# A four-layer network and its gradients on one core: a float32 second operand for the derivative, dS transposes placed anew, identity transposes where layers meet

## The chip, the cores and the metric

The kernel runs on one core of a Trainium2 chip, in one launch. The metric is the device time in microseconds; the time before is the median of four runs.

## The reference

Four residual layers, A, B, A, B, over a sequence of S = 2048 rows of D = 640 in bfloat16, with H = 32 heads of 20. The two A layers share their weights, and so do the two B layers. The kernel returns the network's output, the gradient of its input, and the gradients of the four weight matrices, given the gradient of the output.

```python
def A(x, wqkv, wo):                      # linear attention
    q, k, v = split(x @ wqkv)            # heads of 20
    phi = lambda t: where(t > 0, t + 1, exp(t)) + 1e-6
    pq, pk = phi(q), phi(k)
    kv = einsum("bhsd,bhse->bhde", pk, v)
    z = einsum("bhsd->bhd", pk)
    o = einsum("bhqd,bhde->bhqe", pq, kv) / (einsum("bhqd,bhd->bhq", pq, z)[..., None] + 1e-6)
    return merge(o) @ wo

def B(x, wqkv, wo):                      # causal softmax attention, window of 256
    q, k, v = split(x @ wqkv)
    s = where((i - j >= 0) & (i - j < 256), einsum("bhqd,bhkd->bhqk", q, k) * 20 ** -0.5, -1e9)
    return merge(einsum("bhqk,bhkd->bhqd", softmax(s), v)) @ wo

x = x + A(layernorm(x), A_wqkv, A_wo)    # layer 0
x = x + B(layernorm(x), B_wqkv, B_wo)    # layer 1
x = x + A(layernorm(x), A_wqkv, A_wo)    # layer 2
x = x + B(layernorm(x), B_wqkv, B_wo)    # layer 3
# returned: x, and by jax.vjp with grad_out: dx, dA_wqkv, dA_wo, dB_wqkv, dB_wo
```

## The kernel before

**Stages.** The sequence is cut into 16 tiles of 128 rows. The order of everything on PE, DVE, ACT and POOL is the order of the program; a hand-written plan gives each step a place (a number of slots), the steps are sorted by it and run slot by slot. DMAs all go through the SP queue, which the compiler orders itself. Measured from the span's start, the stages are: the forward pass up to about 688 us; the core of layer 3's gradients, 689 to 1160; layer 2's linear gradients ("linear stage"), 1163 to 1296; the core of layer 1, 1296 to 1768; layer 0's linear gradients mixed with the products for the weight gradients, to 2040; the rest of the weight gradients.

**PLACES.** One table holds the places. `f1`, `f2`, `f3` are steps of the forward pass (normalisation, dense products, features); `bf` is what goes before a core's chunk (`plan_before`: the product of the incoming gradient with Wo, its mask by the softmax's denominator, and the transposes `dT` of L796 and their copies L797); `bh` is what goes behind it (`plan_behind`: the transposes of dq, dk, dv by DMA, the product with the weights, the layer norm's gradient `ln` and `ln2`, the next layer's `dn`, L874 to L904, and the products `outer`); `l2` is one tile of the linear stage (`plan_linear`); `n1` starts layer 1's core inside the linear stage of layer 2. `xx` and `bd` have an entry for each of 32 units and are described next.

**The core.** A core goes through 8 chunks of two tiles; a chunk has 32 units (a tile, four heads, two of them at a time). In each step of `core_step`, a new unit's scores `s` are made (PE, 32-row products, L138 like all products) and its `e = exp(s)` (ACT, L662), masked by POOL (L674, L678); the unit three steps back gets `dp` (PE) and `ds = dp * e` (DVE, L665); the unit four steps back has its `ds` transposed; and the unit seven steps back (`lag`) enters the accumulators `acc` (PE), which read `ds`, `e` and the transposed `dsT`. The transposes take one of two ways. By PE: six transposes into a PSUM tile `flip` (L685) and one copy to `dsT`, on ACT (L690) or DVE (L692). By DMA: one DMA transpose, issued by SP at L108 as soon as `ds` is there. Which way is decided by

```python
    def by_dma(n):
        return n >= 64 and PLACES["bd"][n % 32] == 1
```

and which engine copies by a running count of both engines' work, `on_act`, whose result `xx` inverts from unit 64 on. `thin` is a number of transposes of the identity matrix (`warm`) that are put into a step ahead of the transposes, so that two successive steps have at least `FULL = 3600` columns of PE work:

```python
            k = min(6, max(0, -((cols[n] + cols[n + 1] - self.FULL) // 128)))
            m = n + 1 if not self.by_dma(n - 3) else n
            thin[m] += k
```

The first 64 units of a core have at least `WARM = (6, 4)` of them; they have no transposes by DMA. The last 12 slots of the forward pass up to `END` have `TAIL = 5` each. After `END` the remaining slots of the forward pass run as `hooks` inside the core's first steps.

**The linear stage.** `plan_linear` is run for 16 tiles, 8 slots apart. Its steps in the order of the entries of `l2`: `load` (five loads for two tiles: `ldn`, `lv`, `lpqk`, `lhn`, `lg`); `turn` of dn, v, pk (PE transposes and a copy, L162 and L165 or L167); `part` twice for each of dn, v, pk (products with the 20x21 blocks of the state, and for dn and v the derivative of phi); `turn_q` (a transpose `dqT<-dqa` by DMA); `turn_kv` twice (PE transposes L983, copies L986, L988); six parts of `dh` (products with the weights, closed on ACT, L1001); `ln` (DVE L1009 and L1011, POOL L1012) and `ln2` (ACT L1018, POOL L1019, and for each second tile the store of `lgn`, which is the gradient handed to the next layer). The derivative `fd`, which is min(pqk - 1e-6, 1), is L969, and its product with the PSUM tile is L971:

```python
                nc.vector.scalar_tensor_tensor(out=f, in0=src("pq" if nm == "dn" else "pk")[:, c * CW:(c + 1) * CW], scalar=-EPS,
                                               in1=self.one.to_broadcast([P, CW]), op0=ALU.add, op1=ALU.min)
                nc.vector.tensor_tensor(out=dst, in0=ps[:, 0:CW], in1=f, op=ALU.mult)
```

Layer 1's first `plan_before` (loads of `g<-lgn`, L772 and L779 to L789, the transposes L796) is woven into the end of that stage, from slot `b0` on.

Of the kernel before, what the change touches and what calls it, by code (L numbers as in the profile page):

```python
# [13 lines left out]
BF = mybir.dt.bfloat16  # L14
F32 = mybir.dt.float32
P = 128
# [5 lines left out]
TT = T // P  # L22
DT = D // P
G = H // 4
# [15 lines left out]

PLACES = dict(
    f1=[0.1, 1.7, 2.5, 6.6, 9.6, 12, 13.2, 14.1, 14.5, 14.6, 14.5, 16.1],
    f2=[-27.5, -23.6, -21.5, -20.6, -19.5, -17.9, -16.5, -15.1, -13.5, -7.8, -6.9, -5.5, -4.7, -3.8, -2.9, 11, 12, 13, 14, 17.6, 22.4, 23.3, 24, 25.1, 26.4, 27.3],
    f3=[-35.7, -30, -26.5, -25, -24, -23.8, -22.5, -18, -16.4, -14, -12.1, -7.4, -6.8, -6, -4.9, -3.5, -1.7, 11.3, 12.4, 13.4],
    bf=[2.1, 3.1, 5.2, 14.9, 17.9, 6.2, 7.8, 10, 14.6, 28.3],
    bh=[13.1, 14.5, 15.5, 17.1, 17.5, 18, 20, 21.2, 25.7, 28.3, 30, 36, 19.1, 20.1, 21.8, 22.5, 23.3, 24.6, 25.2, 27.5, 30.5, 31.7, 33, 35, 41.5, 43, 2.2, 8.3, 9.5, 12, 18.9, 34.5],
    l2=[-10.4, -1.3, 0.6, 1.2, 1.9, 3.2, 4.6, 6.2, 7, 7.5, 5, 8, 8.3, 10.2, 11.8, 14, 14.4, 15.4, 16, 16.2, 18.7],
    n1=[9.7, 0.5, 3.3, 3.6, 5.3, 9, 3, 4.7, 5.4, 5.6, 24],
    xx=[1, 1, 0, 0, 0, 0, 1, 1, 0, 0, 0, 0, 0, 1, 0, 0, 1, 0, 0, 0, 0, 0, 0, 1, 0, 0, 1, 0, 0, 0, 1, 0],
    bd=[0, 0, 1, 0, 0, 0, 1, 0, 0, 0, 0, 0, 0, 1, 1, 0, 0, 1, 1, 0, 1, 0, 1, 0, 1, 0, 1, 1, 0, 1, 1, 0])  # L50


class Kern:
    def __init__(self, ctx, tc, x0, A_w, A_wo, B_w, B_wo, grad, outs):
        self.ctx, self.tc = ctx, tc
        self.nc = nc = tc.nc
        self.W = dict(A=A_w, B=B_w)
        self.Wo = dict(A=A_wo, B=B_wo)
        self.grad = grad
        self.out_x4, self.out_gx, dWA, dWoA, dWB, dWoB = outs  # L60
        self.dW = dict(A=dWA, B=dWB)
        self.dWo = dict(A=dWoA, B=dWoB)
        self.serial = 0

        dram = ctx.enter_context(tc.tile_pool(name="dram", bufs=1, space=bass.MemoryType.DRAM))
        const = ctx.enter_context(tc.tile_pool(name="const", bufs=1))

        def d(name, shape, dt=BF):
            return dram.tile(shape, dt, name=name)

        self.hn = [d(f"hn{l}", [T, D]) for l in range(4)]
        self.dq = [d(f"dqkv{l}", [T, QT]) for l in range(4)]
        self.o = [d(f"o{l}", [T, D]) for l in range(4)]
        self.x2 = d("x2", [T, D])
        self.WTA, self.WoTB = d("WTAt", [P, NF * D]), d("WoTBt", [P, DT * D])
        self.x0 = x0
        self.gs = [d(f"g{l}", [T, D]) for l in range(3)] + [grad]
        self.sv = {}
        for l in (0, 2):
            self.sv[l] = dict(pqk=d(f"pqk{l}", [T, 2 * D]), v=d(f"v{l}", [T, DA]),  # L80
                              dn=d(f"dn{l}", [T, DA]))
        for l in (1, 3):
            self.sv[l] = {k: d(f"{k}{l}", [TT, P, 3, G * P]) for k in ("s", "T")}

        self.ident = const.tile([P, P], BF, name="ident")
        make_identity(nc, self.ident)
        self.bm = const.tile([KB, HB, HA], BF, name="bm")
        nc.gpsimd.memset(self.bm, 1.0)
        nc.gpsimd.affine_select(out=self.bm, in_=self.bm, compare_op=ALU.is_ge, fill=0.0, base=0,
                                pattern=[[-DH, HB], [0, HA]], channel_multiplier=1)  # L90
        nc.gpsimd.affine_select(out=self.bm, in_=self.bm, compare_op=ALU.is_ge, fill=0.0, base=DH - 1,
                                pattern=[[DH, HB], [0, HA]], channel_multiplier=-1)
        self.mhalf = const.tile([P, 1], F32, name="mhalf")
        nc.gpsimd.memset(self.mhalf, -0.5)
        self.rs = [const.tile([P, TT], F32, name=f"rs{l}") for l in range(4)]
        self.r = [const.tile([P, TT, H], F32, name=f"r{l}") for l in range(4)]
        self.mz = {l: const.tile([KB, 6, KA], BF, name=f"mz{l}") for l in (0, 2)}
        self.mzT = {l: const.tile([KA, 6, KB], BF, name=f"mzT{l}") for l in (0, 2)}
        self.one = const.tile([P, 1], BF, name="one")
        nc.gpsimd.memset(self.one, 1.0)  # L100
        self.dmz = const.tile([KB, 6, KA], BF, name="dmz")
        self.dmzT = const.tile([KA, 6, KB], BF, name="dmzT")
        self.macc = const.tile([KB, 6, KA], F32, name="macc")
# [133 lines left out]
    def forward(self, st):  # L237
# [48 lines left out]
        B1, B3, F = 138, 302, 6  # L286
        END = B3 + G * TT
        plan = []
# [15 lines left out]
        c1, c3 = 118, B1 + 144  # L304
# [36 lines left out]
        slots = [[f for a, f in plan if int(a) == n] for n in range(int(plan[-1][0]) + 1)]  # L341

        def run(n):
            u, fs = None, slots[n]
            if B1 <= n < B1 + G * TT:
                if n == B1:
                    for f in fs:
                        f()
                    fs = []
                u = self.f_scores(st, *divmod(n - B1, G), X[1])  # L350
            elif B3 <= n < END:
                u = self.f_scores(st, *divmod(n - B3, G), X[3])
            for f in fs:
                f()
            if END - 12 <= n < END:
                self.warm(self.TAIL, st.ps.tile([P, 8, P], BF, name="warm", tag="m"))
            if u is not None:
                self.f_masks(*u)
                st.pend.append((l0(n), *u))
            if len(st.pend) > (st.behind if u is not None else 0):  # L360
                self.b_pv(st, *st.pend.pop(0))

        def l0(n):
            return 1 if n < B3 else 3
        for n in range(END):
            run(n)
        st.pSs.close()
        return [lambda n=n: run(n) for n in range(END, len(slots))], keep

    def f_scores(self, st, t, g, X):  # L370
# [263 lines left out]
        return n >= 64 and PLACES["bd"][n % 32] == 1  # L634

    WARM = (6, 4)
    TAIL = 5
    FULL = 3600

# [505 lines left out]
    def core(self, st, l, g_out, B, hooks):  # L1145
# [37 lines left out]
        for n in range(64):  # L1183
            thin[n] = max(thin[n], self.WARM[n // 32])
        n = 0
# [36 lines left out]
    def passes(self):  # L1222
# [5 lines left out]
        st = S()  # L1228
        with ExitStack() as rest:
# [17 lines left out]
            left3 = self.core(st, 3, self.gs[2], st.core, hooks)  # L1247
# [3 lines left out]
            left3 = left3[8:]  # L1251
# [13 lines left out]
            plan = [(a, lambda f=f: f and f()) for a, f in enumerate(left3)] + [(20, next_pools)]  # L1265
# [9 lines left out]
                self.core_slabs(1, B)  # L1275
            b0 = base + 8 * (TT - 1) + PLACES["n1"][0]
            plan.append((b0, begin))
            fs = self.plan_before(st, 1, 0, B, (PLACES["n1"][1:6], PLACES["n1"][6:11]), -10, True)
            plan += [(b0 + a, f) for a, f, *_ in fs if a < 20]
            hooks = self.slots([(a - 20, f) for a, f, *_ in fs if a >= 20], 8)  # L1280
# [51 lines left out]
            with ExitStack() as es, ExitStack() as le:  # L1332
# [8 lines left out]
                X, plan = {}, []  # L1341
# [70 lines left out]
```

The softmax here doesn't subtract the row's maximum and nothing guards it: scores larger than these inputs give would overflow.

## Time and profile before

| | |
|---|---|
| Median of four runs | 2255.18 us (2252.42 to 2258.45) |
| The profiled execution | 2253.89 us, its span 2252.2 us |
| PE busy | 2077.6 us |
| DVE, ACT, POOL busy | 1454.4, 1357.6, 1092.4 us |
| Identity transposes in the core (`thin`, L173) | 906 |
| Identity transposes at the forward pass's end (`warm`, L173) | 60 |
| dS transposes on PE (L685) / by DMA | 1944 / 156 |

PE is TensorE's matmul, PEld its weight load, DVE VectorE, ACT ScalarE, POOL GpSimd, SP the queue of DMA issues. In the slices each digit is a fortieth of the span, in tenths; PEclk is the clock granted to TensorE in tenths of full speed. In a table of windows each row is one stretch: its length, busy time and instruction count of each engine, the granted clock, the mean busy share of the 16 DMA engines, and GB/s. In the waits a row reads: engine and line, what it waited for, microseconds in total, times, the longest. In the groups: line, engine, operation, names and shapes, count, then busy time in us and mean ns of one, then idle time before.

### The profile page before, as it was taken

The numbers are of one execution on the slowest core, as the hardware profiler recorded it, in microseconds if no ns is written. First come the engines' busy times: TensorE is split into PE (matmuls) and PEld (weight loads), VectorE is DVE, ScalarE is ACT, GpSimd is POOL, SyncE is SP. The second block draws the span as 40 slices with busy tenths as digits, with TensorE's granted clock in tenths as the row PEclk, the third lists the DMA queues.
The fourth block names the chain that finished last, engine by engine and source line by source line (L and its number), as shares of the span: only waits on it lengthen the run. The fifth ranks groups of instructions, "written<-read, shape, count | busy, mean of one in ns | idle before, by whom it ended". The sixth has DMA issues, their size and how long they took to land. (4 is left out here: it accounts for less than half of the span.)

```text
span 2252.2 us, 76829 instructions
## 1 busy us (share of the span) xinstructions
PE 2077.6 (92%) x32061; PEld 1693.2 (75%) x32061; DVE 1454.4 (65%) x2934; ACT 1357.6 (60%) x2109; POOL 1092.4 (49%) x1888
## 2 busy tenths in 40 slices
PE   7889998899989999998979889999988899999999
PEld 5667776577767877777757678777776788889998
DVE  6778885777744788887749858788776245550000
ACT  5467887377776888887737668888876233430000
POOL 2046665156666677777634456777774312220000
PEclk9999999999999999999999989999999999999999
DMA  7488785698879598998799733999997998857753
GB/s 260 142 232 231 224 223 152 159 223 217 205 211 235 151 183 202 211 206 185 157 282 263 203 97 101 205 211 205 202 183 171 270 292 248 247 165 199 201 143 90
DMA packets 721357, 449.50 MB, mean 200 GB/s; under 512 B 461296, under 2 KB 697840, under 8 KB 720624
## 3 DMA queue, kind: packets, MB, share of 16 engines
q1 hardware_dynamic: 721008, 444.58, 78.2%
q8 instruction: 251, 4.11, 0.8%
q14 instruction: 98, 0.80, 0.1%
HBM read 213.09 MB, written 149.82 MB: 161 GB/s over the span
## 5 line engine op out<-in xcount | busy, mean ns | idle before, releaser
L665 DVE TENSOR_TENSOR ds<-dp,e 128x768 bf16<-128x768 f32 (+2 forms) x512 | 463.9, 906 | 175.1 <-PE s L138 61.7
L662 ACT ACTIVATE e<-s 128x768 bf16<-128x768 f32 (+2 forms) x512 | 395.6, 773 | 137.5 <-PE s L138 105.1
L385 ACT ACTIVATE eT<-sT 128x1536 bf16<-128x1536 f32 (+2 forms) x256 | 351.1, 1372 | 130.7 <-PE sT L138 129.3
L138 PE MATMUL wg<-rhs,lhs 128*128 128x240 bf16 (+1 forms) x3840 | 374.4, 256 | 8.3 <-DMA lhs<-o 6.9
L138 PEld LDWEIGHTS <-lhs 128*128 128x128 bf16 x3840 | 337.8, 98 | 23.3 <-DMA lhs<-o 8.1
L674 POOL TENSOR_SCALAR_AFFINE_SELECT e<-e 128x256 bf16<-128x256 bf16 x512 | 208.3, 409 | 249.4 <-ACT e L662 244.0
L138 PEld LDWEIGHTS <-dqT 128*128 128x128 bf16 x1920 | 171.1, 98 | 63.2 <-issue 10.4
L391 POOL TENSOR_SCALAR_AFFINE_SELECT eT<-eT 128x512 bf16<-128x512 bf16 x256 | 162.9, 637 | 108.9 <-ACT eT L385 107.2
L138 PE MATMUL acc<-slabqs,ds 128*128 128x20 bf16 x2880 | 210.1, 172 | 1.4 <-ACT dq L744 0.5
L138 PE MATMUL dp<-slabvT,dT 32*128 32x384 bf16 (+2 forms) x1024 | 167.8, 320 | 44.5 <-DVE ds L665 39.6
L138 PE MATMUL acc<-ds,e 128*128 128x20 bf16 x2880 | 208.1, 171 | 0.0
L678 POOL TENSOR_SCALAR_AFFINE_SELECT e<-e 128x256 bf16<-128x256 bf16 x448 | 197.3, 440 | 0.0
L138 PEld LDWEIGHTS <-ds 128*128 128x128 bf16 x2880 | 188.0, 96 | 11.8 <-issue 3.5
L138 PEld LDWEIGHTS <-e 128*128 128x128 bf16 x2880 | 170.2, 96 | 10.8 <-issue 1.8
L1012 POOL TENSOR_TENSOR dh<-dh,lg 128x640 f32<-128x640 f32 x32 | 51.5, 1610 | 256.7 <-DVE s L1009 256.7
L685 PE MATMUL flip<-ident,ds 128*128 128x128 bf16 x1944 | 169.8, 221 | 3.3 <-DVE ds L772 1.2
L138 PE MATMUL s<-slabkT,slabqT 32*128 32x384 bf16 (+2 forms) x1024 | 167.9, 323 | 4.6 <-ACT dT L797 3.3
L1094 DVE CAST wr<-wg 128x240 bf16<-128x240 f32 (+1 forms) x72 | 27.2, 377 | 222.1 <-PE wg L138 213.6
L1092 ACT CAST wr<-wg 128x240 bf16<-128x240 f32 (+1 forms) x48 | 16.3, 339 | 254.8 <-PE wg L138 223.4
L138 PE MATMUL dense<-WB,hnT 128*128 128x320 bf16 x960 | 166.2, 305 | 3.4 <-DVE o L459 2.0
L138 PE MATMUL dense<-WTA,dqT 128*128 128x320 bf16 x960 | 162.9, 301 | 1.4 <-DMA dqT<-dqa 1.0
L138 PE MATMUL acc<-slabks,dsT 128*128 128x20 bf16 x2880 | 147.2, 171 | 12.7 <-DMA dsT<-ds 12.6
(176 smaller groups left out, 4604.4 us busy)
## 6 DMA issues: line engine op xcount, KB each, us to landing
rhs<-dqkv SPq DMA_DIRECT2D x64, 480.0 KB, 5.0
s<-s SPq DMA_DIRECT2D x32, 768.0 KB, 3.9
T<-T SPq DMA_DIRECT2D x32, 768.0 KB, 3.9
dqkv<-dq SPq DMA_DIRECT2D x16, 960.0 KB, 5.7
dqkv<-dqa SPq DMA_DIRECT2D x32, 480.0 KB, 4.6
slabkT<-T SPq DMA_DIRECT2D x56, 256.0 KB, 4.5
slabvT<-T SPq DMA_DIRECT2D x56, 256.0 KB, 4.1
slabks<-s SPq DMA_DIRECT2D x56, 256.0 KB, 3.8
```

Of the source, the lines that this page charges most:

```text
L138: return self.nc.tensor.matmul(out, lhsT=lhsT, rhs=rhs, start=start, stop=stop, skip_group_check=True, **kw)
L385: nc.scalar.activation(e[:, :, 0:nb * P], s[:, :, 0:nb * P], ACT.Exp)
L391: nc.gpsimd.affine_select(out=dg, in_=dg, compare_op=ALU.is_ge, fill=0.0, base=0, pattern=[[0, 4], [1, P]], channel_multiplier=-1)
L662: nc.scalar.activation(u.e[:, :, 0:u.cw], s[:, :, 0:u.cw], ACT.Exp)
L665: nc.vector.tensor_tensor(out=d.ds[:, :, 0:d.cw], in0=d.dp[:, :, 0:d.cw], in1=d.e[:, :, 0:d.cw], op=ALU.mult)
L674: nc.gpsimd.affine_select(out=dg, in_=dg, compare_op=ALU.is_ge, fill=0.0, base=0, pattern=[[0, 2], [-1, P]], channel_multiplier=1)
L678: nc.gpsimd.affine_select(out=fr, in_=fr, compare_op=ALU.is_ge, fill=0.0, base=-1, pattern=[[0, 2], [1, P]], channel_multiplier=-1)
L685: nc.tensor.transpose(ps[:, 3 * j + i, :], f.ds[:, j, i * P:(i + 1) * P], self.ident)
L1012: nc.gpsimd.tensor_tensor(out=x["dh"], in0=x["dh"], in1=L["g"][:, i, :], op=ALU.add)
L1092: nc.scalar.copy(o[:, 0:w], ps[:, 0:w])
L1094: nc.vector.tensor_copy(o[:, 0:w], ps[:, 0:w])
```

## The change

Three things change at once.

1. The table `PLACES`: entries of `f2`, `f3`, `bf`, `bh`, `l2`, `n1`, and the flags `xx` and `bd`. `bd` has 15 units of 32 by DMA in the place of 13: units 6 and 17 go back to PE, units 5, 11, 16 and 28 go to DMA, so that 26 to 30 are all by DMA. Counted in the program: 180 DMA transposes of dS (156 before), 1800 PE transposes of dS (1944), 940 `thin` transposes (906).
2. `self.one`, the second operand of L969, is float32 in the place of bfloat16.
3. `HOLD`: identity transposes, 8 in a slot, in three places where one layer's work meets the next: the slots after the end of the forward pass (the first steps of layer 3's core), the slots around the beginning of layer 2's linear stage (from four before the end of layer 3's left-over steps to three behind it), and seven slots from `b0` + 3.95 at the end of that stage. The first two entries of `HOLD` are 0 and put nothing in. The program has 228 `warm` transposes, 60 before.

```diff
 PLACES = dict(
-    f2=[-27.5, -23.6, -21.5, -20.6, -19.5, -17.9, -16.5, -15.1, -13.5, -7.8, -6.9, -5.5, -4.7, -3.8, -2.9, 11, 12, 13, 14, 17.6, 22.4, 23.3, 24, 25.1, 26.4, 27.3],
-    f3=[-35.7, -30, -26.5, -25, -24, -23.8, -22.5, -18, -16.4, -14, -12.1, -7.4, -6.8, -6, -4.9, -3.5, -1.7, 11.3, 12.4, 13.4],
-    bf=[2.1, 3.1, 5.2, 14.9, 17.9, 6.2, 7.8, 10, 14.6, 28.3],
-    bh=[13.1, 14.5, 15.5, 17.1, 17.5, 18, 20, 21.2, 25.7, 28.3, 30, 36, 19.1, 20.1, 21.8, 22.5, 23.3, 24.6, 25.2, 27.5, 30.5, 31.7, 33, 35, 41.5, 43, 2.2, 8.3, 9.5, 12, 18.9, 34.5],
-    l2=[-10.4, -1.3, 0.6, 1.2, 1.9, 3.2, 4.6, 6.2, 7, 7.5, 5, 8, 8.3, 10.2, 11.8, 14, 14.4, 15.4, 16, 16.2, 18.7],
-    n1=[9.7, 0.5, 3.3, 3.6, 5.3, 9, 3, 4.7, 5.4, 5.6, 24],
-    xx=[1, 1, 0, 0, 0, 0, 1, 1, 0, 0, 0, 0, 0, 1, 0, 0, 1, 0, 0, 0, 0, 0, 0, 1, 0, 0, 1, 0, 0, 0, 1, 0],
-    bd=[0, 0, 1, 0, 0, 0, 1, 0, 0, 0, 0, 0, 0, 1, 1, 0, 0, 1, 1, 0, 1, 0, 1, 0, 1, 0, 1, 1, 0, 1, 1, 0])
+    f2=[-26.3, -23.6, -21.5, -20.6, -19.5, -17.4, -16.5, -15.4, -13.5, -7.8, -6.9, -5.5, -4.8, -3.8, -2.9, 11, 12.5, 13, 14, 17.6, 22.4, 23.2, 24.1, 25.1, 26.5, 27.3],
+    f3=[-35.7, -29.4, -26.6, -25, -24, -23.8, -22.2, -18, -16.4, -15, -12.1, -7.7, -6.8, -6, -4.4, -3.4, -1.7, 11.3, 12.4, 13.4],
+    bf=[2.6, 3.1, 5.2, 12.9, 17.7, 6.7, 9.3, 10.5, 16.6, 29.3],
+    bh=[13.1, 14.6, 15.8, 17.1, 17.5, 18, 20, 21.2, 25.7, 28.3, 30, 36, 19.6, 20.1, 21.8, 22.5, 23.3, 24.6, 25.2, 27.5, 30.5, 31.7, 33, 35, 41.5, 43, 2.2, 8.3, 10.5, 11, 19.9, 34.5],
+    l2=[-12.4, -0.6, -3.8, 2.7, 1.3, 3.1, 4.6, 6.2, 6.7, 7.6, 5.3, 8.1, 8.1, 9.7, 11.8, 14, 14.7, 16, 17.1, 18.9, 20.5],
+    n1=[9.6, 0, 2.4, 3.7, 4.5, 6.1, 0.5, 5.5, 5.8, 6.6, 24.3],
+    xx=[1, 1, 1, 0, 0, 1, 1, 1, 0, 1, 0, 0, 0, 1, 0, 0, 0, 0, 0, 0, 0, 0, 0, 0, 1, 0, 1, 0, 0, 0, 1, 0],
+    bd=[0, 0, 1, 0, 0, 1, 0, 0, 0, 0, 0, 1, 0, 1, 1, 0, 1, 0, 1, 0, 1, 0, 1, 0, 1, 0, 1, 1, 1, 1, 1, 0])
...
-        self.one = const.tile([P, 1], BF, name="one")
+        self.one = const.tile([P, 1], F32, name="one")
...
+            for a, b, k in ((c1 - 2, B1, self.HOLD[0]), (B1 + G * TT, B3, self.HOLD[1]), (END, len(slots), self.HOLD[2])):
+                if a <= n < b and k:
+                    self.warm(k, st.ps.tile([P, 8, P], BF, name="warm", tag="m"))
             for f in fs:
...
     WARM = (6, 4)
+    HOLD = (0, 0, 8, 8, 8)
     TAIL = 5
...
+            def hold(k):
+                self.warm(k, st.ps.tile([P, 8, P], BF, name="warm", tag="m"))
+            plan += [(len(left3) + a, lambda: hold(self.HOLD[3])) for a in range(-4, 4)]
+            plan += [(b0 + a + 0.95, lambda: hold(self.HOLD[4])) for a in range(3, 10)]
             fs = self.plan_before(st, 1, 0, B, (PLACES["n1"][1:6], PLACES["n1"][6:11]), -10, True)
```

## The prediction

> **What bounds the kernel now.** I read the head of the page and the slices first.
>
> ```profile
> span 2252.2 us, 76829 instructions
> ...
> PE 2077.6 (92%) x32061; PEld 1693.2 (75%) x32061; DVE 1454.4 (65%) x2934; ACT 1357.6 (60%) x2109; POOL 1092.4 (49%) x1888
> ...
> PE   7889998899989999998979889999988899999999
> ...
> PEclk9999999999999999999999989999999999999999
> DMA  7488785698879598998799733999997998857753
> ```
>
> PE carries 92% of the span and every slice. Its clock falls in one slice only, the one where layer 2's gradients hand over to layer 1's core. Next, the table of windows: a steady chunk of each core, the first 10.2 us of layer 3's core, the linear stage of layer 2, the first 13.7 us of layer 1's core, the linear stage of layer 0.
>
> ```profile
> core 0: us, PE busy (x) PEld busy (x) DVE busy (x) ACT busy (x) POOL busy (x), PEclk, DMA share, GB/s
> 876.27:931.81 55.54, 51.48 (x988) 41.14 (x986) 44.87 (x67) 44.95 (x76) 42.63 (x83) 1.00 0.95 203
> 688.70:698.90 10.20, 8.94 (x77) 5.75 (x78) 3.18 (x8) 4.21 (x8) 4.25 (x9) 0.50 0.71 162
> 1185.00:1283.00 98.00, 92.29 (x1066) 73.62 (x1063) 92.45 (x175) 67.44 (x137) 44.78 (x32) 1.00 0.86 234
> 1296.30:1310.00 13.70, 10.10 (x76) 6.67 (x75) 3.51 (x8) 5.31 (x10) 6.84 (x10) 0.50 0.21 62
> 1483.61:1538.77 55.16, 51.48 (x988) 41.13 (x986) 44.89 (x68) 44.97 (x76) 42.65 (x83) 1.00 1.03 213
> 1850.00:2040.00 190.00, 190.00 (x2042) 169.69 (x2041) 99.18 (x193) 73.67 (x153) 46.22 (x30) 1.00 0.74 209
> ```
>
> So PE sets the chunks (51.5 of 55.5 us) with 4 us of gaps, and the DMA engines stand near 1.0 beside it. Both cores begin at half clock. In layer 0's linear stage PE has no gap at all. Third, the waits: 850 to 1070 us (four lines), then 1283 to 1312 us (one line), then PE's alone from 1290 to 1312 us (one line).
>
> ```profile
> PE dp L138 <- DVE ds L665: 10.7, 27, 0.9
> PE acc L138 <- DMA dsT<-ds: 5.2, 5, 2.9
> DVE ds L665 <- DMA dsT<-ds: 5.0, 2, 3.4
> DVE ds L665 <- ACT dsT L690: 1.8, 3, 0.6
> ...
> DVE ds L665 <- DMA g<-lgn: 9.4, 1, 9.4
> ...
> PE s L138 <- ACT dT L797: 3.3, 1, 3.3
> ```
>
> In the core, PE waits for `ds`, seldom for a DMA transpose. At the hand-over it waits for `dT`, and `ds` for the store of `lgn`. Fourth, the groups by form.
>
> ```profile
> L690 ACT COPY dsT<-flip 128x768 bf16<-128x768 bf16 x158 | 126.4, 800 | 0.3
> L969 DVE SCALAR_TENSOR_TENSOR fd<-lpqk,one 128x320 bf16<-128x320 bf16 x128 | 101.5, 793 | 0.0
> L692 DVE COPY dsT<-flip 128x768 bf16<-128x768 bf16 x134 | 73.3, 547 | 0.0
> ```
>
> L969 takes 793 ns on average, 482 ns in the median (the tile view), so (793 - 482) x 128 = 40 us of it is standing still.
>
> **Transposes of dS (bd, xx, bf, bh).** There are 8 chunks of 32 units per core and `bd` counts from unit 64, so it acts on 6 chunks of each core. Per chunk 15 units instead of 13 go by DMA: 144 PE transposes go in the program, and the fill-up to FULL adds 34, net -110. Eight transposes back to back took 0.62 us in the timeline (L983 at 1283.82), the first 0.22 (its group's mean), so 0.057 us each: -6.3 us, 0.5 a chunk, as far as PE bounds. Copies: with the new `xx`, ACT makes 7 instead of 11 (-4 x 0.800 = -3.2 us), DVE 10 instead of 8 (+2 x 0.547 = +1.1 us, to 46.0 of 55.5). DVE stays under PE; what I charge it is later `ds`, what ACT gives back is earlier `e`, and I set these against each other. SP gets 24 issues of 1.2 us more, 2.5 us a chunk. Three further DMAs (the second `turn`, `store`, `load_o`) move by one unit of 1.73 us, and the entries of `bf` by up to two; they keep their order towards the units that read them, so I charge nothing, and if one came late the price is a wait like `PE acc <- DMA`, about 1 us a chunk. Taken: -0.5 us a chunk, **-6 us**. Good bound: half of PE's wait for `ds` (10.7 us over 4 chunks' 220 us, so 1.35 a chunk) goes too, -1.8 a chunk, -22 us. Bad bound: the DMA rival below.
>
> **Identity transposes (HOLD).** The first two entries are 0. The program gains 168: 56 as layer 3's core opens, 64 where layer 2's gradients begin, 48 where they end. At 0.057 us all of them cost 9.6 us if nothing covers them, twice that at half clock. Each group also takes a buffer of the pool `m`, so it waits until the tile that had it is read (three buffers in the forward pass), and PE's queue behind it waits along: up to a DVE copy of 0.547 us for each of 7.
> - Core 3: at 688.7 us PE falls to half clock after a window in which it waits for the POOL masks (L395, up to 0.7 us a time). The 10.2 us at half clock hold matmuls that PE shows busy for 8.94 us. Twice the clock saves at most half of that, 4.5 us, less where s, e and the masks are the chain. Taken -2.5 (bounds -4.5 and +4, the waits for buffers).
> - Start of layer 2: PE waits 3.5 us for `dn` of L904 at 1163.7, and 6.8 us then run at half clock. Gain up to 3.4, but the 16 transposes between the outer products are on the chain (0.9) and so are the rest in part. Taken 0 (-2.5 to +2).
> - End of layer 2: 48 transposes are 2.7 us in a stretch where PE stands idle more than that; they put the drop off but `ds` still waits to 1303.7 us. Taken 0 (-2 to +2).
>
> Whether transposes hold the clock: from 1129.0 to 1132.4 us PE ran 30 transposes and 6 products, and the clock stayed at 1.00. The Trainium skill, "TensorE: Matmul & The Clock Gate", Part 4, says that transposes do not count as PE activity for the full clock; this row speaks against it. By the page the gain at core 3 would fall out and the sum would be 2.5 less.
>
> **Hand-overs (l2, n1).** Before, ACT's copy `dT` stands behind the last `lna` (L1018), and PE waits 3.3 us; in the new order it stands ahead of them. The whole wait goes; next is the wait for `lgn`: POOL L1012 1.40, L1019 1.54, then a store of 3.4 us, and `ln` now comes 2.7 and `ln2` 1.8 slots later in the last tile, while n1 starts 0.1 earlier. PE's 3.3 us are therefore not all gain. Taken **-3** (bounds -6 and +3).
> The SP queue: `lg` must wait for POOL L1012 of the tile before, and with `ln` 2.7 slots later the transpose `dqT`, queued right behind it, goes out about as late as before, when it stood behind the store of `lgn` (10.9 + 2.8 against 10.7 + 2.7 slots): 0.3 slot later in every second tile, where PE waited for `dqT` 1.0 us in all. 7 x 0.3 = 2, taken **+1** (0 to +3).
>
> **Forward (f2, f3).** Dense groups, normalisations and copies change places by 0.1 to 1.2 slots; nothing is added. Taken **-1** (-4 to +3).
>
> **Derivative's operand.** `one` is [128, 1], read with step 0, so in F32 the bytes of the other two streams are unchanged. Where POOL is silent (74 of 128) L969 takes 0.48; the other 54 end 0.35 us after the POOL operation beside them (L1012, L1019). Two SBUF inputs with an f32 one also stand still for POOL: L874 took 825 ns at its shortest and 1044 in the median. L772, with an f32 operand of step 0 from SBUF and one from PSUM, took 490 and never waited. So I expect 482 ns and the same waits: **0**. The skill's "GPSIMD Engine Reference" (section 8, Key points) lists two SBUF inputs among the cases of contention; L874 agrees. Bounds: the rival, and +0.3 us on those 55 in layer 2's stage that now stand directly before `kv` (2 to 4 us).
>
> Sum: -6 - 2.5 + 0 + 0 - 3 + 1 - 1 + 0 = -11.5. The profiled run took 2253.9 (span 2252.2 and 1.7 around it), 1.3 under the median of 2255.2; 2253.9 - 11.5 = **2242**.
>
> **Rivals.**
> - *F32 ends the standing still.* Then 46.9 us - 55 x 0.482 = 20.4 us of DVE time go in the window 1185 to 1283. PE's gaps there are 98 - 92.3 = 5.7 us; over the 16 tiles (7.235 us each, 116 us) 6.7. About 7 more, **2235**. In layer 0's stage PE is full, so nothing. For it: of the readers with step 0, L969 alone stands still, and it alone has only bf16 from SBUF. Against: L874.
> - *Slower: the DMA engines become the bound of the cores.* A transpose moves 196,608 bytes, at the chunk's 203 GB/s 0.97 us; 24 of them are 23 us, and units 26 to 30 now come five in a row, at 1.73 us each. It replaces the -6: -11.5 + 6 + 23 = +17.5, **2271**. It decides when landing (median 3.7 us, longest 7.4) passes the four units, 6.9 us, after which PE uses the tile. For it: shares of 0.95 and 1.03. Against: PE waited only 5 times, 5.2 us, in 220 us.
> - *The holds do not hold, or stand in the way.* -2.5 is lost, and the 112 outside core 3's idle time cost 112 x 0.057 = 6.4: -11.5 + 2.5 + 6.4 = -2.6, **2251**.
>
> **How the numbers follow.** Forecast 0.50, F32 0.15, DMA 0.13, holds 0.22. 0.2% (4.5 us) is about what a measurement of this kernel can tell from no change. Faster: 0.47 of the forecast, F32 0.15, and 0.10 of the holds, 0.72. Same: 0.03 and 0.07, 0.10. Slower: DMA 0.13, 0.05 of the holds, 0.18. The range: the good bounds together, -22 - 4.5 - 3 - 1 - 4 = -34.5, give about 2220 (under it 0.05); above, half of the DMA rival's loss over the forecast, up to 2262, so that some 0.1 is left out. The likeliest case alone holds 2230 to 2250.
>
> **What would show it.** Right: windows at 688.7 with the clock at 1.00; chunks of 54.5 to 55.2 us; no wait of `s` for `dT`; L969 at 482 ns with a mean near 790. Wrong: the wait of `acc` for `dsT` above 9 us in 220 us and chunks over 56 (the DMA rival); a mean of L969 near 490 (the F32 rival); the first 10 us of core 3 at 0.50 and PE gaps around the holds (the third).

## The result, and the profile after

The changed kernel takes 2259.3 us (median of 52 runs, 2249.2 to 2271.2) where the kernel before takes 2254.6 (77 runs, 2243.7 to 2265.3): ratio 1.0022, 95% interval 1.0015 to 1.0030. It is 4.7 us slower; the forecast was 11.5 us faster. The profiled execution took 2267.3 us, 8 above the median of its kernel, so its whole span isn't to be set against the other; what repeats in it (a tile's period, the waits of one stage) is. First the head of its page and two of its rows of slices.

```profile
span 2265.6 us, 77002 instructions
...
PE 2085.1 (92%) x32119; PEld 1699.8 (75%) x32119; DVE 1453.5 (64%) x2952; ACT 1326.9 (59%) x2067; POOL 1094.8 (48%) x1888
...
PE   7899998899989999999888899999998899999999
...
PEclk9899999999999999999989999999999999999999
```

PE's row has lost a tenth in the 22nd slice (9 before, 8 now), which is 1189 to 1246 us, in the linear stage of layer 2. The clock's row has its 8s in the 2nd and the 21st slice. The 24th, where layer 1's core opens and where the row of before had its only 8, now shows 9: 6.8 us at half clock, 13.7 before. The windows, for the same stretches as before (first 10.2 us of core 3, a chunk of core 3, layer 2's linear stage, a chunk of core 1, layer 0's stage):

```profile
core 0: us, PE busy (x) PEld busy (x) DVE busy (x) ACT busy (x) POOL busy (x), PEclk, DMA share, GB/s
695.60:705.80 10.20, 9.95 (x136) 7.61 (x137) 6.32 (x15) 5.08 (x12) 5.22 (x11) 1.00 1.05 223
...
904.20:959.47 55.27, 51.20 (x978) 40.76 (x976) 45.64 (x68) 42.07 (x72) 42.62 (x83) 1.00 1.00 221
1199.00:1296.00 97.00, 81.81 (x954) 66.75 (x953) 88.39 (x157) 58.80 (x120) 39.23 (x28) 1.00 0.78 219
1525.83:1581.49 55.66, 51.23 (x978) 40.79 (x976) 45.71 (x70) 41.97 (x72) 42.50 (x83) 1.00 0.99 222
...
1860.00:2050.00 190.00, 190.00 (x2035) 168.85 (x2034) 80.82 (x193) 75.79 (x153) 47.99 (x30) 1.00 0.74 209
```

Core 3 starts at full clock, and the core's engines moved as the sum had it (ACT 45.0 to 42.1, DVE 44.9 to 45.6 a chunk). PE's busy time fell by 0.28 and 0.25 us a chunk, half of the sum's 0.5, and these two chunks, 55.27 and 55.66 us, are no shorter than the two of before, 55.54 and 55.16. The linear stage of layer 2 is the one that broke: PE does 954 instructions in 97 us where it did 1066 in 98. From one `ln` to the next a tile takes 8.06 us, before 7.24, in every one of its middle tiles. Twelve tiles make 10 us, more than the whole loss. Before, DVE sets this period: from 1207 to 1280 us it waits for nothing, and its instructions follow one another from `ln` to `ln`. PE's costliest wait in this stretch names the link. First the kernel before, then the changed one:

```profile
PE dense L138 <- DVE dqa L971: 3.3, 8, 0.5
```
```profile
PE flip L987 <- DVE dqa L975: 11.3, 9, 1.3
```

The timeline of one tile shows the chain behind it.

```profile
1231.39 0.82 DVE L1013 CUSTOM_DVE_ANT_0 lna<-dh,lhn 128x640 f32<-128x640 f32 x1
...
1232.31 1.70 POOL L1016 TENSOR_TENSOR dh<-dh,lg 128x640 f32<-128x640 f32 x1 [4.10 <-DVE s L1013]
...
1234.73 1.53 POOL L1023 TENSOR_TENSOR lgn<-dh,lna 128x640 bf16<-128x640 f32 x1 [0.72 <-ACT lna L1022]
1234.87 1.75 DVE L973 SCALAR_TENSOR_TENSOR fd<-lpqk,one 128x320 bf16<-128x320 bf16 x1
...
1236.72 0.49 DVE L975 TENSOR_TENSOR dqa<-dense,fd 128x320 bf16<-128x320 f32 x1
...
1237.26 0.72 PE L987 MATMUL flip<-ident,dqa 128*128 128x128 bf16 x10 [1.26 <-DVE dqa L975]
...
1237.82 0.84 PE L138 MATMUL dense<-WTA,dqT 128*128 128x320 bf16 x5
...
1238.50 0.31 PE L138 MATMUL dense<-mzT,dnT 126*128 126x120 bf16 x3
...
1238.70 0.53 ACT L1005 ACTIVATE dh<-dense,rs 128x320 f32<-128x320 f32 x1
1238.84 0.49 DVE L975 TENSOR_TENSOR dqa<-dense,fd 128x320 bf16<-128x320 f32 x1 [0.21 <-PE dense L138]
...
1239.44 0.82 DVE L1013 CUSTOM_DVE_ANT_0 lna<-dh,lhn 128x640 f32<-128x640 f32 x1
```

Read it as a ring. `ln` of one tile lets POOL begin; ACT and POOL finish its `ln2` (place 20.5). Behind it comes the derivative of v's second half, two tiles on (6.2 + 16 = 22.2). This 0.48 us instruction starts 0.14 us behind POOL's addition and ends 0.35 us after it, 1.75 us long. Its product goes to the kv transposes of that tile, for which PE waits 1.26 us. Behind them on PE stands the last part of `dh` of the tile between: its place is 17.1, and the transposes of the tile after it are at 8.1 + 8 = 16.1. ACT closes that part, and `ln` of the tile between follows. (The product of dn's first half, next on PE, is late with it: DVE waits 0.21 us for it at 1238.84, and is done when ACT is.) From `ln` to `ln` that is 8.06 us. Before, that part of `dh` had place 16 and stood ahead of the transposes, so the ring was open.

The three groups:

```profile
L694 ACT COPY dsT<-flip 128x768 bf16<-128x768 bf16 x114 | 91.5, 803 | 0.2 <-PE flip L689 0.2
L973 DVE SCALAR_TENSOR_TENSOR fd<-lpqk,one 128x320 bf16<-128x320 bf16 x128 | 87.5, 684 | 0.0
L696 DVE COPY dsT<-flip 128x768 bf16<-128x768 bf16 x154 | 84.2, 547 | 0.0
```

Over the whole program the derivative stands still less than before: (684 - 481) x 128 = 26 us, where it was 40. But the two linear stages went opposite ways. In layer 0's it fell from 19 to 1 us, where PE is busy for 190.00 of 190.00 us either way. In layer 2's it grew. The group there, before (1185 to 1283 us) and in the changed kernel (1207 to 1296 us):

```profile
L969 DVE SCALAR_TENSOR_TENSOR fd<-lpqk,one 128x320 bf16<-128x320 bf16 x55 | 46.9, 853 | 0.0
```
```profile
L973 DVE SCALAR_TENSOR_TENSOR fd<-lpqk,one 128x320 bf16<-128x320 bf16 x44 | 41.8, 951 | 0.0
```

With four derivatives a tile, that is 1.9 us of standing still in each tile where it was 1.5, in the order of the engine that sets the period.

### The profile page after: what moved, and what is told of

Same layout as the page of the kernel before. It is cut to its first block, busy times and chain, and to the rows that moved or that the text cites. A ratio compares the mean times of both kernels' runs of the same rounds, so it can differ in the third digit from the quotient of the medians.

```text
span 2265.6 us, 77002 instructions
## 1 busy us (share of the span) xinstructions
PE 2085.1 (92%) x32119; PEld 1699.8 (75%) x32119; DVE 1453.5 (64%) x2952; ACT 1326.9 (59%) x2067; POOL 1094.8 (48%) x1888
## 5 line engine op out<-in xcount | busy, mean ns | idle before, releaser
L689 PE MATMUL flip<-ident,ds 128*128 128x128 bf16 x1800 | 158.6, 222 | 1.8 <-DVE ds L776 1.1
L138 PE MATMUL dense<-WTB,dqT 128*128 128x320 bf16 x960 | 157.4, 304 | 0.7
```

The source lines that it names most:

```text
L138: return self.nc.tensor.matmul(out, lhsT=lhsT, rhs=rhs, start=start, stop=stop, skip_group_check=True, **kw)
L689: nc.tensor.transpose(ps[:, 3 * j + i, :], f.ds[:, j, i * P:(i + 1) * P], self.ident)
```

## The experiments

**The linear stage's order.** Four kernels on one chip. `after_l2_old`, the changed kernel with

```diff
-    l2=[-12.4, -0.6, -3.8, 2.7, 1.3, 3.1, 4.6, 6.2, 6.7, 7.6, 5.3, 8.1, 8.1, 9.7, 11.8, 14, 14.7, 16, 17.1, 18.9, 20.5],
+    l2=[-10.4, -1.3, 0.6, 1.2, 1.9, 3.2, 4.6, 6.2, 7, 7.5, 5, 8, 8.3, 10.2, 11.8, 14, 14.4, 15.4, 16, 16.2, 18.7],
```

> The changed kernel with the linear stage's places (l2) of before; all else stays. Theory 1 (order): in the new order the derivative of v's second half (L973) stands behind the last POOL addition of ln2 and ahead of the transposes for kv, so its standing still is on the chain, 8.06 us a tile where it was 7.24; with the old places the period is 7.24 again, PE's wait of flip L987 for dqa L975 (13.9 us in 89) is gone, and the time is 11 to 13 us under the changed kernel, about 7 us under the kernel before. Theory 2 (the float32 operand makes the stage slow): the period stays near 8 and the time near the changed kernel's, within 3 us.

2253.9 us, ratio to the kernel before 0.9997 (0.9980 to 1.0014), period 7.24. The period came back as theory 1 has it; the time came back to the kernel before and not 7 us below it: about 5.6 us under the changed kernel, where 11 to 13 were expected. `before_l2_new` is the kernel before with the new lines `l2` and `n1`:

> The kernel before with the new l2 and n1 only, operand bfloat16, no holds. Theory 1: period 8.06 us, 11 to 13 us over the kernel before. Theory 2: period near 7.24, within 3 us of the kernel before. The hand-over at the end of the stage: if the new n1 saves the wait of s for dT, 3 us less than the period alone would give.

2263.5 us, ratio 1.0038 (1.0020 to 1.0055), about 8.6 us slower (11 to 13 were expected), period 8.06, with the same wait in the same stretch (1207 to 1280 us) of this kernel:

```profile
PE flip L983 <- DVE dqa L971: 11.3, 9, 1.3
```

So the new order does it with the bfloat16 operand and without holds. `before_f32` changes one word of the kernel before:

```diff
-        self.one = const.tile([P, 1], BF, name="one")
+        self.one = const.tile([P, 1], F32, name="one")
```

> The kernel before with the derivative's second operand in float32 and nothing else. Theory 1: L969 at 0.48 us alone and still standing behind POOL, mean near 0.79, time within 2 us of the kernel before. Theory 2: slower by 5 us or more, period over 7.24. The forecast's F32 rival: mean of L969 near 0.49, 7 us faster.

2253.4 us, ratio 0.9991 (0.9975 to 1.0007), period 7.24. The median and the mean of this kernel are those of before to a nanosecond (482 and 793 there):

```profile
L969 DVE SCALAR_TENSOR_TENSOR fd<-lpqk,one x128: 479/483/1785, 1170.3 to 2012.3; 128x320 bf16<-128x320 bf16 x128
```
```profile
L969 DVE SCALAR_TENSOR_TENSOR fd<-lpqk,one 128x320 bf16<-128x320 bf16 x128 | 101.6, 794 | 0.0
```

The operand does nothing, neither to the duration nor to the wait for POOL. `after_ln_early` was my first idea of the mechanism:

```diff
-    l2=[..., 14, 14.7, 16, 17.1, 18.9, 20.5],
+    l2=[..., 14, 14.7, 16, 17.1, 17.2, 18.9],
```

> The changed kernel with two numbers of l2 changed, ln from 18.9 to 17.2 and ln2 from 20.5 to 18.9, so that the two POOL additions meet the derivatives of dn and of v's first half and leave v's second half alone. Theory 1: period 7.2 to 7.4, time 8 to 12 us under the changed kernel. If it is another of l2's places (turn of v at -3.8, the loads) that makes the stage slow, the period stays near 8.

The expectation missed: 2266.5 us, ratio 1.0053 (1.0028 to 1.0077), and the period rose to 8.45. The second half of v's derivative was indeed free (0.48 us), but two others stood still, 1.11 and 1.24 us long, ahead of it in DVE's order, and `ln` still came after the kv transposes: over 1207 to 1280 us DVE waits nine times for ACT's `dh`, up to 1.2 us. So it isn't the one instruction: the ring is still closed, and everything between `ln` and the transposes is in it. Hence the next one, `after_dh_early`, which leaves `ln` and `ln2` and opens the ring elsewhere:

```diff
-    l2=[..., 14, 14.7, 16, 17.1, 18.9, 20.5],
+    l2=[..., 14, 14.4, 15.4, 16, 18.9, 20.5],
```

> The changed kernel with three numbers of l2 changed back: the last three parts of dh at 14.4, 15.4 and 16 (changed kernel 14.7, 16, 17.1); ln and ln2 stay at 18.9 and 20.5. After the first runs the theory is narrower: with 17.1 the last part of dh stands on PE behind the kv transposes of the next tile (8.1 + 8 = 16.1), and these wait for the derivative of v's second half, which waits for POOL's addition of ln2, which waits for ln, which waits for that last part of dh: a closed loop over one tile. With 16 the loop is cut: period 7.2 to 7.5, time 8 to 11 us under the changed kernel, although the derivative of v still stands behind POOL as long as before. Rival: the standing still itself, ahead of the kv transposes, sets the period, wherever dh stands: 8 us as before.

Ratio 1.0004 (0.9986 to 1.0021), 2256.2 us, period 7.62. The derivative of v's second half still took 1.74 us, and yet PE's wait over 1207 to 1280 us fell from 11.3 to

```profile
PE flip L987 <- DVE dqa L975: 4.8, 9, 0.5
```

Half of the lost 0.82 us a tile comes back by three numbers. The expectation, 7.2 to 7.5, was a little too good. The other half is DVE's own. In this kernel it waits only once over 1207 to 1280 us (0.6 us), so its own order sets the period again; and its second and third derivative of a tile take 1.09 and 1.74 us, where they took 1.11 and about 1.3 before. Over ten tiles the standing still is 1.86 us a tile here and 1.46 before: 0.40 more, and the period is 0.38 longer. The wait for POOL was tried next: `after_no_lgn_add` takes the second POOL operation away, and with it leaves `dh` and the incoming gradient out of `lgn`.

```diff
-            nc.scalar.activation(x["a"], L["hn"][:, i, :], ACT.Identity, bias=x["s1"], scale=x["s2"])
-            nc.gpsimd.tensor_tensor(out=L["gn"][:, i, :], in0=x["dh"], in1=x["a"], op=ALU.add)
+            nc.scalar.activation(L["gn"][:, i, :], L["hn"][:, i, :], ACT.Identity, bias=x["s1"], scale=x["s2"])
```

> The changed kernel without the second POOL addition of the linear stages (L1023): ACT writes its layer norm term straight into lgn and the incoming gradient is left out of it. So the derivative of v's second half finds POOL silent. If the wait for POOL is a link of the loop: this derivative takes 482 ns, the period falls from 8.06 by the 1.27 us that it stood still, to 6.8 to 7.2 (PE needs about 6.5). If it is the order alone, the period stays at 8.06.

One run: period 6.70 in ten of fourteen tiles (8.06 less the 1.27 expected is 6.79), 7.5 to 8.8 in the other four, 7.09 on average; and the longest derivative of all 128 fell from 1809 to 1135 ns:

```profile
L973 DVE SCALAR_TENSOR_TENSOR fd<-lpqk,one x128: 478/482/1135, 1166.9 to 2001.8; 128x320 bf16<-128x320 bf16 x128
```

So the wait for POOL and the order both have a part in the period; either one taken away shortens it. This kernel takes the wait out of the ring and out of DVE's own order at once, so it can't tell the two apart. `after_dh_early` does: 0.44 us a tile for the ring, 0.38 for the longer standing still.

| kernel | period in layer 2's stage, us | layer 0's stage, first to last `ln`, us | ratio to before |
|---|---|---|---|
| before | 7.24 | 194.9 | 1 |
| changed | 8.06 | 191.4 | 1.0022 |
| after_l2_old | 7.24 | 193.5 | 0.9997 |
| before_l2_new | 8.06 | 191.3 | 1.0038 |
| after_ln_early | 8.45 | 194.1 | 1.0053 |
| after_dh_early | 7.62 | 190.8 | 1.0004 |
| after_no_lgn_add | 6.70 | 191.5 | (one run) |

(For `after_no_lgn_add` the table has the period of most tiles.) The third column looks like a second effect of the same table. A tile of layer 0's stage takes 13.14 us either way, but its first and last `ln` stand closer with the new `l2`: 191.2 us on average in the five profiles that have it there, 193.4 in the nine with the old. It is no gain: from the last `ds` of core 1 to the end of the span, the same five take 517.8 us and the nine 516.9. What the order costs in layer 2 can be read from the last `ds` of core 3 to the first `ds` of core 1: 189.2 us in the four profiles with the new order there (187.5 to 190.8), 181.5 in ten with the old (178.7 to 184.9). These 7.7 us are less than 12 x 0.82 = 10, in part since the core's first `ds` comes sooner behind the last `ln`, 7.6 to 8.2 us in the place of 8.1 to 10.5.

**The core's tables.** `before_core` is the kernel before with the new lines `bf`, `bh`, `xx` and `bd`.

> The kernel before with bd, xx, bf and bh of the changed one, nothing else. The forecast's step: 6 us faster, chunks half a microsecond shorter. Theory from the waits of the first runs (PE's wait of acc for dsT by DMA grew from about 6 to 10 us in 325 us, its wait of dp for ds fell by 1): what the PE transposes give is taken back by the wait for the DMA transposes, so within 3 us of the kernel before. DMA rival in full: 15 us slower or more.

2249.1 us, ratio 0.9965 (0.9947 to 0.9983), 7.9 us faster. The forecast's step was right in size, and my second thought wrong about the time. PE's wait of `acc` for `dsT`, before (850 to 1070 us) 5.2, is in the changed kernel (855 to 1075)

```profile
PE dp L138 <- DVE ds L669: 11.8, 25, 0.9
...
PE acc L138 <- DMA dsT<-ds: 5.8, 7, 1.9
```

One profile says little here; taken together they show that this wait does grow: from unit 64 on, over both cores, it is 16.1 us on average in the eleven profiles with the new tables (12.2 to 19.3) and 12.2 in the six with the old (10.2 to 15.0). PE's wait for `ds` fell by 2.4. From the first to the last `ds` of each core, both together, the eleven took 850 to 862 us, mean 856, and the six 859 to 862, mean 860. These 4 us don't lie where the sum had them. Units 64 to 223, five chunks of each core, take 559.7 us with the new tables and 559.5 with the old; the first 64 units of both cores are 1.4 shorter (six of the eleven have the holds too, one of the six), the last 32 are 2.7 shorter. Why, and where the rest of the 7.9 is, these runs don't show.

**The holds.** `before_hold` is the kernel before with `HOLD` and its two insertions; `after_no_hold` is the changed kernel with

```diff
-    HOLD = (0, 0, 8, 8, 8)
+    HOLD = (0, 0, 0, 0, 0)
```

> The kernel before with HOLD = (0, 0, 8, 8, 8) and nothing else. Holds worth their forecast: 2 to 3 us faster, full clock at the start of layer 3's core. Holds in the way: 2 to 6 us slower. Holds that only move the clock's drop: within 2 us of the kernel before and as much half clock in sum.

Ratio 0.9993 (0.9975 to 1.0010), 2255.5 us.

> The changed kernel with all five entries of HOLD at 0. The forecast had the holds worth 2.5 us at the start of layer 3's core and nothing at the other two places: then this run is about 2.5 us over the changed kernel, its first 10 us of the core at half clock. Rival (they stand in the way): 2 to 6 us under the changed kernel, the gaps of the two hand-overs shorter.

Ratio 1.0013 (0.9994 to 1.0032), 2258.1 us, against 1.0022 with the holds. Neither way anything that these runs can tell from nothing. At core 3 the profiles show that the holds keep the clock: the first 32 units of core 3 have a stretch at half clock in all ten kernels without them and in none of the seven with them. But the first 64 units took 95.6 us on average without and 94.9 with them, so the clock was worth some 0.7 us, and among the eleven kernels with the new tables it is 95.2 and 95.0; and from the last `ds` of core 3 to the second tile of the linear stage it was 67.9 without and 69.6 with them, 1.7 lost, though the two ranges overlap (66.2 to 70.3, 68.6 to 70.4). At the other two places the clock is another matter: from the last `ds` of core 3 to layer 2's first `ln` the half clock is 12.4 us on average without the holds and 13.2 with them, and around the opening of layer 1's core it falls from 11.9 to 6.8, which the time doesn't show. Since core and holds might disturb each other, `core_and_hold` has both and nothing else, and `l2_old_no_hold` is the changed kernel with the old `l2` and `HOLD` at 0:

> The kernel before with the core's tables (bd, xx, bf, bh), which alone gave a ratio of 0.9965, and HOLD = (0, 0, 8, 8, 8); f2, f3, l2, n1 and the operand are those of before. The two were alone worth -7.9 and about -1.6 us. If they add: 8 to 10 us under the kernel before. If the holds take the core's gain back (in the four profiles with both, layer 3's core took 429.7 to 434.9 us, with the new tables and no holds 425.8 and 427.2, because chunks 3 and 6 had a late dS transpose by DMA): within 3 us of the kernel before, core 3 at 430 us or more.

2248.4 us, ratio 0.9970 (0.9955 to 0.9985).

> The changed kernel with l2 of before and HOLD at 0: what is left are the core's tables, f2, f3, n1 and the operand. If the holds take the core's gain back: 6 to 9 us under the kernel before, core 3 at 426 to 428 us. If it is f2, f3 or n1: within 3 us of the kernel before, as the changed kernel with l2 of before and the holds was (0.9997).

2249.5 us, ratio 0.9978 (0.9962 to 0.9994). The holds take nothing back from the core: the first result says so, and the lateness of chunks 3 and 6 that I had seen in some profiles was spread, since core 3 took 430.5 us without holds here, too.

**The forward pass.** `before_forward` is the kernel before with the new lines `f2` and `f3`.

> The kernel before with f2 and f3 of the changed one only. Forecast's step: 1 us faster. In the profiles the forward pass took 690 to 696 us with either table, so within 2 us of the kernel before; if f2 and f3 lose what the core gains, 4 us slower or more.

2253.6 us, ratio 0.9995 (0.9979 to 1.0012): nothing.

**Do the terms add?** `core_and_l2` is the kernel before with the new `bf`, `bh`, `xx`, `bd`, `l2` and `n1`; `before_n1` has the new `n1` alone.

> The kernel before with the core's tables (alone 0.9965) and l2 and n1 of the changed kernel (alone 1.0038). If the two add: ratio 1.000 to 1.001, the time within 2 us of the kernel before. If the core's gain is lost beside the new l2: 1.003 or more, 7 us over the kernel before. The period of layer 2's stage is 8.06 either way.

2257.6 us, ratio 1.0014 (1.0001 to 1.0028). Closer to the sum of the two (1.0003) than to a loss of the core's gain.

> The kernel before with n1 of the changed one only (the opening of layer 1's core at the end of layer 2's stage). Forecast's step: 3 us faster, no wait of s for dT. From the profiles (last tile to the first ds of the core 26.3 us before, 25.1 to 25.3 in all kernels with the new n1): 1 us faster. If n1 takes the core's gain: 4 us slower or more.

2256.0 us, ratio 1.0001 (0.9985 to 1.0017): the 3 us of the forecast aren't there. A least-squares fit of the twelve ratios (these eleven with exact sets of edits, and the change itself), each weighted by its interval, puts the core's tables at -6.6 us (plus or minus 2.4), `l2` at +7.9 (2.6), the holds at +0.9 (2.1), `f2` and `f3` at +0.9 (2.9), `n1` at +1.6 (2.7) and the operand at -0.1 (2.9); the sum is +4.6, the change +4.7. The intervals take the ratios as independent, though kernels of one chip share the runs of before.

**A version that beats both.** `core_l2_split` is the kernel before with the core's tables and the new `l2` in layer 0's stage alone:

```diff
-        a = PLACES["l2"]
+        a = PLACES["l2" if l == 2 else "l0"]
```

> The kernel before with the core's tables, and with the new l2 in layer 0's linear stage only (layer 2's keeps the old one); no holds. The loop over one tile cannot close in layer 0's stage, where products for the weight gradients fill PE and a tile takes 13.14 us either way; the profiles show its 15 tiles at 191 us with the new l2 and 193 to 195 with the old. So 2 to 3 us better than the core's tables alone: 8 to 11 us under the kernel before, ratio 0.995 to 0.9965.

2249.7 us, ratio 0.9973 (0.9958 to 0.9988), period 7.24, layer 0's tiles 191.0 us. It is faster than both kernels. It isn't seen to beat the core's tables alone (0.9965): the 2 to 3 us that layer 0's stage was to give aren't found.

## Why the prediction was wrong, point by point

- **Linear stage (`l2`): the step that failed.** The prediction took the hand-over at -3 and the SP queue at +1, and looked in `l2` only for what moves at its two ends; the period of the tiles between it left as it was, at no cost. It did see that derivatives which stand still would now stand before the kv transposes, and put 2 to 4 us on it as a bound, outside the sum, counting 0.3 us on each of those. It never followed the tile's steps around a period: whether what waits for the derivative leads back to `ln`. It does, since the last part of `dh` went from 16 to 17.1, past the next tile's transposes at 16.1. In its place the runs showed a period of 8.06 us where it was 7.24: 0.44 by this ring, 0.38 by longer standing still in DVE's own order, which already set the period. The measured term is +7.9 us.
- **Core (-6): size right, its working not borne out.** -7.9 alone, -6.6 in the fit. The sum had 0.5 us a chunk from PE's 110 fewer transposes at 0.057. In the chunks shown PE's busy time fell by half of that, the chunks of 54.5 to 55.2 us didn't come, and five chunks of each core together take as long as before. What shows is at the two ends of the cores; that it adds up to about 6 is in part luck. Whether PE's or ACT's relief brings it wasn't separated. The DMA rival didn't come: the share near 1.0 stayed near 1.0 with 24 more transposes, and PE waits 4 us more for them over both cores.
- **Holds (core 3 -2.5, others 0): mechanism right, size wrong.** The transposes held the clock, as the row of 1129 us had said. But of the 2.5 us only 0.7 are seen, 1.7 are lost where layer 2 begins (taken at 0), and over all the fit has +0.9 (2.1). So the half clock over 10.2 us was hardly what bounded the start of core 3; what did (the POOL masks, the copies) no run separated. (The prediction has 56 of the transposes at core 3 and 48 where layer 2 ends; in the profile it is 48 and 56.) The Trainium skill, "TensorE: Matmul & The Clock Gate", Part 4, which has transposes not count for the full clock, differs from these seven profiles (in `before_hold` transposes are all that was added), and the measurement decides.
- **Hand-over (-3): not found.** The wait of `s` for `dT` is gone from PE's waits, as said. What is late next is ACT's `e` (1.6 us at most) and the store of `lgn`, for which `ds` still waits:

```profile
DVE ds L669 <- DMA g<-lgn: 6.4, 1, 6.4
...
PE s L138 <- ACT e L666: 2.1, 2, 1.6
```

  (waits from 1295 to 1335 us of the changed kernel, all engines and PE's alone). With `n1` alone the time doesn't move.
- **Operand (0): right**, for the reason given: the row of L874 was the right one, and the F32 rival is out. "The same waits" held for the operand, but not for the new order.
- **Forward (-1): within the measurement of nothing.**
- **The rivals.** The rival on the slower side was the wrong one. The right one stood in the paragraph on the operand, as a bound of 2 to 4 us, too small and outside the sum. The range's own working doesn't come out either: half of the DMA rival's loss over the forecast is 2242 + 14.5 = 2257, not 2262, and the good bounds named with the terms add up to -41 (-22, -4.5, -2.5, -2, -6, -4), not -34.5.

## What to carry to other kernels

When steps of a software pipeline are moved, write down each engine's order over one period and look for rings: a step that waits for the next tile's work, which waits for the tile before. An engine that is busy without a gap from one tile to the next is a ring by itself, and its stalls lengthen it. The sum of an engine's stalls over a whole program says nothing of that: here it fell from 40 to 26 us, in a stage where PE set the pace and nothing was gained, while it grew in the stage where DVE set the pace, and that one's period grew by 11%. So read stalls stage by stage, beside what bounds each. And don't take two marks that come closer together for time saved: layer 0's `ln`s did, and the end of the program came no sooner.

## What the runs showed of the hardware

- The float32 type of a second operand with step 0 changed neither the 0.48 us of the derivative nor its wait for a POOL operation, which it ends 0.35 us after. With that POOL operation taken away, the derivative of v's second half takes 0.48 us and not 1.75.
- Identity transposes, 8 in each of six steps beside other work, kept TensorE at 1.00 over the first 10.2 us of core 3, where it had been at 0.50, and the first 64 units were 0.7 us shorter on average, with spreads of 2 us on either side.
- With a DMA share near 1.0 in the chunks, 24 more DMA transposes (156 to 180) lengthened PE's waits for them by 4 us over both cores (12.2 to 16.1), and the cores took no longer.
- From one execution to the next the changed kernel varies by about 20 us (2249 to 2271), so single profiles tell periods and orders, not 5 us of a span.
